# Loading k in natural key order, moving a mask to TensorE, and regrouping an output phase, in an attention + MoE kernel

## The chip, the cores and the metric

The kernel runs on one core of a Trainium2 chip. The metric is the time of one execution on the device, in microseconds (us). The lowest and the highest run of one kernel in one call lie 0.15% (e12b) to 0.83% (the changed kernel again) apart here, in e7b 1.1%; each run also lists the mean clock that was granted to TensorE. A change counts as faster or slower only from 2% on.

Engine names: PE is TensorE (matmuls) and PEld its weight loads, DVE is VectorE, ACT is ScalarE, POOL is GpSimd, and SP is SyncE. "Hardware queue" means a DMA queue fed by ACT or SP, and "software queue" the one fed by POOL. PSUM is the memory that the matmuls write; a "bank" is here one [128, 512] f32 slice of it, and the tiles named `s4` have four. A "stretch" is a piece of the execution between two marks. "First MoE matmul" always means the start of the first matmul on `w_in`.

## The reference

For 8 batches and 8 heads of size 64, 32 global and 512 local tokens attend. Global queries see all keys; local queries see the global keys and the local keys at a distance of at most 32. The result, transposed to tokens x 512, goes through a two-layer MLP. Cut to what matters:

```python
s_g = scale * q_g @ concat([k_g, k_l]).T                  # global rows
out_g = softmax(s_g) @ concat([v_g, v_l])
s_ll = where(abs(i - j) <= 32, scale * q_l @ k_l.T, -1e9) # banded local scores
s_l = concat([scale * q_l @ k_g.T, s_ll])
out_l = softmax(s_l) @ concat([v_g, v_l])
x = concat([out_g, out_l]).transpose(0, 2, 1, 3).reshape(B * S, H * D)
h = x @ w_in                                              # 512 -> 2048
return (h / (1 + exp(-1.702 * h))) @ w_out                # 2048 -> 512
```

## The kernel before

The program is scheduled by hand: every engine runs its instructions in the order in which they are written here. A "quad" is four heads of one batch, so there are 16 quads. After an opening, in which batch 0 gets its attention, MoE phases of 64 matmuls ("h" phases, `x @ w_in`) alternate with output phases of 64 matmuls ("o" phases, `g @ w_out`). The attention of the next batch is woven into these phases, mostly into the output phases. The first output phase and the second MoE phase are written out separately, and later ones come from one function.

The parts that the change touches (cuts marked with `# ...`):

```python
# k in 4-token rows; its partition order makes four loads of 64 KB per quad
kf = k_l.rearrange("b (u j) (c r t) d -> b j r u c (t d)", j=4, c=4, t=4)
def load_k(b, u, j):
    nc.gpsimd.dma_start(out=loaded[b][0][32 * j : 32 * j + 32, u], in_=kf[b, j][:, u])

# small global tiles of batch 0 in f32, cast later; v in two pieces (turned by 32 partitions)
def load_g32(b, names, hold=False, eng=None):
    for name, s in (("q", qgf), ("k", kgf), ("v", vgf)):
        if name in names:
            t = g32[b, name] = consts.tile([128, 2, D], F32, name="g32%s%d" % (name, b))
            if hold:                       # the load waits for this memset's engine
                nc.vector.memset(t[:, :, 0:1], 0.0)
            # ... issue on eng or nc.sync

q32 = ld.tile([128, 16 * D], F32, name="q32", bufs=1)
nc.scalar.dma_start(out=q32, in_=qf[0][:, 0])
load_g32(0, "qk")
load_g32(0, "v", eng=nc.scalar)            # small v tile: issued at once, on ACT's queue
for j in range(4):
    load_k(0, 0, j)
# ...
def Tk(self, cs=(0, 1, 2, 3)):             # k transpose: contiguous in, contiguous out
    # ...
    nc.vector.transpose(self.kT[:, cs], rk[:, cs])
def M(self, rnd, lo=0, hi=LW):             # mask: multiply exp(scores) by 0/1
    # ...
    nc.vector.tensor_mul(e, e, mask[:, rnd : rnd + 1, lo:hi].to_broadcast([128, 4, hi - lo]))
def R(self):                               # reciprocals of the sums: two transposes and a reciprocal
    # ...
def XL(self, h):                           # scaled outputs of the local rows -> x
    nc.vector.tensor_mul(self.x[:, 2 * self.u + h, :], self.st[1 + h], self.st["rs"])
def G(self):                               # global rows -> xG, needed only by the last MoE phase
    # ... reciprocal, multiply, transpose, reading self.st["og"]
```

The opening and the first output phase (`a` and `c` are two quads of one batch; S scores, X exp, M mask, ekU/U value matmuls, Gm the matmuls of the global rows, osteps the output matmuls):

```python
a.S(0); a.X(0); a.S(1, split=True, warm=4); a.X(1)   # written one per line in the kernel
c.ext(); cast_g32(0, "v"); c.Tk(); a.K(); a.XK(); a.M(0); c.Tq(); c.gg(); c.S(0); c.X(0); a.M(1)
# ...
a.ekU(1, 3); c.S(1); c.X(1, halves=True); a.ekU(2, 4); a.U(1); a.U(2); a.Gm(); c.M(0); a.XL(0)
# ...
# first output phase, its last third:
osteps(0, (3, 0)); a.U(1); a.U(2); c.S(1); a.Gm(); c.M(0); a.XL(0); a.XL(1)
c.X(1); c.M(1); c.eg(); a.G()
osteps(0, (3, 1), (3, 2))
c.UG(); c.RXG()                            # value matmuls, reciprocals, x, then G
osteps(0, (3, 3))
```

The softmax here doesn't subtract the row's maximum and nothing guards it: scores larger than these inputs give would overflow.

## Time and profile before

| Stage, read from the timeline of TensorE | us |
|---|---|
| start to the first MoE matmul | 20.19 |
| first MoE phase | 14.22 |
| first output phase, to the first matmul of the second MoE phase | 22.67 |
| second MoE phase, to the third one's start (with its output phase) | 36.02 |
| each later MoE phase with its output phase | 34.41 |
| span of the profiled execution | 310.7 |
| time, median of four runs (312.46 to 314.58) | 312.97 |

The page's busy row gives the engine, its busy time, its share of the span and its instructions:

```profile
PE 302.8 (97%) x3257; PEld 148.6 (48%) x3257; DVE 210.4 (68%) x463; ACT 167.3 (54%) x254; POOL 80.0 (26%) x131
```

TensorE is busy nearly all the time, so the change looks for its gain in the two stretches that do not run at the pace of the later phases: the opening, and the first output phase.

The timeline of before in the opening, TensorE only. Columns: start, duration, engine, line, operation with out<-in, tile, shape, type, count, and in brackets the idle time before it and its releaser:

```profile
8.49 1.04 PE L162 MATMUL s<-warm 128*128 128x512 bf16 x4
...
14.14 0.40 PE L367 MATMUL ov<-ek,rvg 32*32 32x512 bf16 x4
...
15.07 1.04 PE L162 MATMUL ov<-warm 128*128 128x512 bf16 x4
...
20.19 1.04 PE L457 MATMUL s<-xL,w_in_sb 128*128 128x512 bf16 x4
```

TensorE does useful work in small groups. The 11 matmuls on the tile `warm` after the first scores (two of their three groups are shown) compute nothing; they fill time in which TensorE would wait for exps and masks. The first value matmuls with global v (`ov<-ek,rvg`) run at 14.14 us.

The DMA view of before for the first 20 us. Columns: out<-in, issuing queue, kind and count, KB of each, and the median us from issue to landing:

```profile
q<-in_q_l_dram ACTq DMA_DIRECT2D x1, 512.0 KB, 3.9
...
g32v<-in_v_g_dram ACTq DMA_DIRECT2D x1, 48.0 KB, 4.2
g32v<-in_v_g_dram SPq DMA_DIRECT2D x1, 48.0 KB, 13.1
```

There are two loads named `g32v` because before also loads batch 1's small tiles early. Batch 0's, issued at 1.3 us, took 4.2 us. The same load for batch 1, issued at 14.1 us when the software queue was full of v and weights (its four 512 KB loads of `w_in`, issued from 10.4 us on, took 11.7 us in the median), took 13.1 us.

DVE's timeline of before at the end of the first output phase:

```profile
53.84 0.16 DVE L426 RECIPROCAL rg<-og 128x1 f32<-128x1 f32 x1
...
54.53 0.67 DVE L412 STREAM_TRANSPOSE sT<-ov 128x512 f32<-128x512 f32 x1
...
55.52 0.71 DVE L416 STREAM_TRANSPOSE rs<-rT 128x512 f32<-128x512 f32 x1
56.34 1.29 DVE L421 TENSOR_TENSOR xL<-ov,rs 128x512 bf16<-128x512 f32 x2
57.55 0.16 DVE L426 RECIPROCAL rg<-og 128x1 f32<-128x1 f32 x1
```

The reciprocal at 53.84 us begins quad a's G, which reads `og` in a bank of its own. The tail of the phase is sT, rT, rs and xL of quad c: xL ends at 57.63 us, 0.55 us after the second MoE phase began at 57.08 us. Quad c's G follows at 57.55 us and holds nobody up.

Finally, the groups of DVE transposes by form in before (busy us and mean ns of one):

```profile
L260 DVE STREAM_TRANSPOSE kT<-rk 128x512 f32<-128x512 f32 x15 | 10.6, 704 | 0.0
L263 DVE STREAM_TRANSPOSE q<-rq 128x512 f32<-128x512 f32 x15 | 10.2, 677 | 0.0
```

### The profile page before, as it was taken

The page shows a single profiled execution, that of the slowest core. Times are in us where ns is not written, and L with a number is a line of the kernel's source. Part 1 is how long each engine was busy: PE and PEld are TensorE (multiplying, and loading weights), DVE is VectorE, ACT ScalarE, POOL GpSimd, SP SyncE. Part 2 cuts the span into 40 slices and gives each one's busy share as a digit, 9 for nine tenths or more (in the row PEclk, how much of TensorE's full clock was granted, in tenths as well). Part 3 has the DMA queues.
Part 4 walks back from the last instruction along what each step waited for, and adds up shares of the span by engine and source line. Part 5 has one row for each costly group of instructions (what it writes and reads, how often), then busy time and mean ns, then how long its engine had stood idle before and what let it go on. Part 6 is the DMA issues. An engine that isn't in the chain of part 4 may idle for free.

```text
span 310.7 us, 7885 instructions
## 1 busy us (share of the span) xinstructions
PE 302.8 (97%) x3257; PEld 148.6 (48%) x3257; DVE 210.4 (68%) x463; ACT 167.3 (54%) x254; POOL 80.0 (26%) x131
## 2 busy tenths in 40 slices
PE   7899999999999999999999999999999999999995
PEld 6444444444554454444454455444454454446653
DVE  7887946869867866776957866776767855574320
ACT  4817465476536744565446735565556652563321
POOL 8822579677146000900045001200000000000000
PEclk9999999999999999999999999999999999999999
DMA  8999999999969212970279113901120012201123
GB/s 154 149 189 207 206 161 193 165 147 129 151 77 168 45 36 61 139 108 12 60 77 169 30 36 71 102 0 31 41 49 23 0 38 55 48 0 29 41 61 76
DMA packets 60099, 27.44 MB, mean 88 GB/s; under 512 B 43296, under 2 KB 51744, under 8 KB 60064
## 3 DMA queue, kind: packets, MB, share of 16 engines
q0 software_dynamic: 51536, 17.11, 50.7%
q1 hardware_dynamic: 7904, 9.12, 11.9%
q10 hardware_dynamic: 624, 0.72, 0.8%
q8 instruction: 25, 0.41, 0.5%
q14 instruction: 10, 0.08, 0.1%
HBM read 35.13 MB, written 8.91 MB: 142 GB/s over the span
## 4 chain that ended last, share of the span: by engine, by line
PE 91%; DVE 3%; ACT 2%; DMA 1%; POOL 1%; issue 0%; ACTq 0%; DVEq 0%; POOLq 0%
PE op L482 37%; PE hp L457 36%; PE s L291 6%; PE ov L389 5%; PE ov L367 3%; DMA rk<-in_k_l_dram 1%; PE s L457 1%; ACT e L322 1%; PE kb L310 1%; DVE e L329 1%; PE op L494 1%; PE s L310 1%; DVE gT L465 1%; PE s L406 1%; POOL rk L84 1%; PE ov L162 1%
## 5 line engine op out<-in xcount | busy, mean ns | idle before, releaser
L482 PE MATMUL op<-w_out_sb,gT 128*128 128x512 bf16 x528 | 121.9, 380 | 0.1
L465 DVE SCALAR_TENSOR_TENSOR gT<-th,hp 128x512 bf16<-128x512 f32 (+1 forms) x140 | 91.1, 655 | 43.0 <-ACT th L464 42.4
L457 PE MATMUL hp<-xL,w_in_sb 128*128 128x512 bf16 x496 | 108.6, 379 | 0.3 <-DVE xL L421 0.3
L464 ACT ACTIVATE th<-hp 128x512 f32<-128x512 f32 (+1 forms) x140 | 79.9, 573 | 43.7 <-PE hp L457 41.2
L457 PEld LDWEIGHTS <-w_in_sb 128*128 128x128 bf16 x576 | 56.1, 98 | 65.1 <-issue 1.2
L482 PEld LDWEIGHTS <-gT 128*128 128x128 bf16 x528 | 49.3, 98 | 56.2 <-issue 3.3
L322 ACT ACTIVATE e<-s 128x1712 bf16<-128x1712 f32 (+2 forms) x32 | 49.6, 1552 | 15.8 <-PE s L406 8.9
L496 ACT ACTIVATE ob<-op 128x512 f32<-128x512 f32 (+2 forms) x35 | 20.5, 585 | 61.6 <-PE op L482 59.1
L97 POOL DMA_DIRECT2D v<-in_v_l_dram x36 | 27.0, 757 | 96.2 <-PE s L406 88.9
L84 POOL DMA_DIRECT2D rk<-in_k_l_dram x64 | 34.9, 557 | 12.3 <-DMA w_in_sb<-in_moe_w_in_dram 4.7
L329 DVE TENSOR_TENSOR e<-e,mask 128x1408 bf16<-128x1408 bf16 (+2 forms) x33 | 28.0, 851 | 6.9 <-ACT e L322 6.7
L412 DVE STREAM_TRANSPOSE sT<-ov 128x512 f32<-128x512 f32 x16 | 11.4, 714 | 31.3 <-PE ov L389 31.3
L291 PE MATMUL s<-q,kT 32*128 32x200 bf16 (+1 forms) x512 | 21.3, 284 | 1.5 <-DVE kT L260 0.9
L421 DVE TENSOR_TENSOR xL<-ov,rs 128x512 bf16<-128x512 f32 x32 | 20.7, 685 | 2.2 <-PE ov L389 0.9
L291 PEld LDWEIGHTS <-kT 32*128 32x128 bf16 x512 | 10.9, 95 | 14.7 <-issue 9.1
L357 ACT ACTIVATE ek<-kb 128x512 bf16<-128x512 f32 x16 | 9.6, 600 | 8.4 <-PE kb L310 8.4
L389 PE MATMUL ov<-e,v 128*32 128x192 bf16 (+1 forms) x512 | 13.1, 240 | 0.0
L416 DVE STREAM_TRANSPOSE rs<-rT 128x512 f32<-128x512 f32 x16 | 11.4, 711 | 0.6
L260 DVE STREAM_TRANSPOSE kT<-rk 128x512 f32<-128x512 f32 (+1 forms) x17 | 11.4, 671 | 0.0
L263 DVE STREAM_TRANSPOSE q<-rq 128x512 f32<-128x512 f32 (+1 forms) x17 | 10.9, 647 | 0.0
L389 PEld LDWEIGHTS <-v 128*32 128x32 bf16 x512 | 9.8, 97 | 2.0 <-issue 2.0
L310 PE MATMUL kb<-q,kgT 32*32 32x512 bf16 x128 | 10.0, 385 | 0.5 <-ACT e L319 0.5
(71 smaller groups left out, 155.5 us busy)
## 6 DMA issues: line engine op xcount, KB each, us to landing
out_dram<-ob SPq DMA_DIRECT2D x132, 64.0 KB, 1.7
rk<-in_k_l_dram POOLq DMA_DIRECT2D x64, 64.0 KB, 4.0
v<-in_v_l_dram POOLq DMA_DIRECT2D x28, 128.0 KB, 4.5
rq<-in_q_l_dram POOLq DMA_DIRECT2D x6, 512.0 KB, 6.7
w_in_sb<-in_moe_w_in_dram POOLq DMA_DIRECT2D x4, 512.0 KB, 11.7
w_out_sb<-in_moe_w_out_dram POOLq DMA_DIRECT2D x4, 512.0 KB, 13.4
rq<-in_q_l_dram POOLq DMA_DIRECT2D x3, 256.0 KB, 7.9
q<-in_q_l_dram ACTq DMA_DIRECT2D x1, 512.0 KB, 3.9
```

Of the source, the lines that this page charges most:

```text
L84: nc.gpsimd.dma_start(out=loaded[b][0][32 * j : 32 * j + 32, u], in_=kf[b, j][:, u])
L97: nc.gpsimd.dma_start(out=vtiles[b % 2][p, s, :, :, :D], in_=vf[b, t][:, hs])
L291: nc.tensor.matmul(ps[j][:, off : off + n * nr], lhsT=self.k[p, 128 * c : 128 * c + 128, e], rhs=self.q[p, t0 : t0 + n, r0 : r0 + nr, e], ...
L322: nc.scalar.activation(e[:, :, lo:hi], self.ps[:, :, lo:hi], AF.Exp, scale=scale)
L329: nc.vector.tensor_mul(e, e, mask[:, rnd : rnd + 1, lo:hi].to_broadcast([128, 4, hi - lo]))
L389: nc.tensor.matmul(ov[32 * j : 32 * j + 32, :].rearrange("p (t r) -> p t r", t=16)[:, :, r0 : r0 + nr], lhsT=lv, rhs=self.E[c // 2][:, j, ...
L421: nc.vector.tensor_mul(self.x[:, 2 * self.u + h, :], self.st[1 + h], self.st["rs"])
L457: nc.tensor.matmul(hp[:, : width(i)], lhsT=w_in_c[:, fc // 8, kc, fc % 8 // 2, :, fc % 2], rhs=(xL[i] if i < B else xG)[:, kc, :], start=( ...
L464: nc.scalar.activation(th[:, :n], hp[:, :n], AF.Tanh, scale=0.851)
L465: nc.vector.scalar_tensor_tensor(gTs[i][:, fc, :n], in0=th[:, :n], scalar=1.0, in1=hp[:, :n], op0=ALU.add, op1=ALU.mult)
L482: nc.tensor.matmul(op, lhsT=gTs[i][:, fc, tci * 128 : tci * 128 + 128], rhs=w_out_sb[:, fc, :], start=(first and fc == 4 * f4), stop=(fc = ...
L496: nc.scalar.activation(ob[:, lo:hi], op[:, lo:hi], AF.Copy, scale=0.5)
```

## The change

The intent has four parts.

1. k is loaded like q, in 16-token rows of 2 KB on the software queue, which makes one load per pair of quads in place of eight. Keys come out in natural order only if the k transpose writes with a step (`"p (r t) -> p t r"`, a step of 16 f32 = 64 bytes).
2. k and q of the first quad come as f32 on the two hardware queues and are cast on chip.
3. In batch 0 the mask becomes a bias (0 or -262144) that an identity matmul adds to the scores in PSUM ahead of the score matmuls, in place of a multiplication after the exp.
4. The first output phase is regrouped so that matmuls of one tile size stand together.

On the way, the small v tile's load moves behind a DVE memset (`hold=True`) on SP's queue, constants move to POOL, and quad 1's loads leave the software queue earlier. The diff has more that the list leaves out: v's loads follow the new order of the keys, the first half of `w_in` comes in four loads in place of two, batch 1's small tiles come on the software queue, and the warm-up matmuls at the very start go from 62 to 40.

The diff, cut to its core:

```diff
-    kf = k_l.rearrange("b (u j) (c r t) d -> b j r u c (t d)", j=4, c=4, t=4)
+    kf = k_l.rearrange("b (u j) (r t) d -> b (j r) u (t d)", j=4, t=16)
 # ... load_k and load_q replaced by two whole loads
-    nc.scalar.dma_start(out=q32, in_=qf[0][:, 0])
-    load_g32(0, "qk")
-    load_g32(0, "v", eng=nc.scalar)
-    for j in range(4):
-        load_k(0, 0, j)
+    load_g32("q", qgf)
+    for eng, f in ((nc.scalar, halves[0]), (nc.sync, halves[1])):
+        eng.dma_start(out=k32[:, f], in_=kf[0][:, 0, f])
+        eng.dma_start(out=q32[:, f], in_=qf[0][:, 0, f])
+    load_g32("k", kgf)
 # ... constants on POOL, the band matrix, identity and bias
-            nc.vector.transpose(self.kT[:, cs], rk[:, cs])
+            nc.vector.transpose(self.kT.rearrange("p (r t) -> p t r", t=16)[:, lo:hi],
+                                loaded[self.b][0][:, self.u].bitcast(F32)[:, 32 * lo : 32 * hi])
+        def B(self, rnd, split=False):
+            # ...
+                for j in range(4):
+                    nc.tensor.matmul(ps[j][:, w : w + 16 * WIN[c][1]], lhsT=ident, rhs=near(bias, c),
+                                     start=(c == 2 * rnd), stop=False, skip_group_check=True)
 # ... opening
+    load_g32("v", vgf, hold=True)
+    cast_g32("k", rkg)
     transpose_g(0, 2, "k")
     load_rest()
+    a.B(0)
+    a.B(1, split=True)
+    a.S(0, added=True, part=0)
+    a.S(0, added=True, part=1)
     a.X(0)
-    a.S(1, split=True, warm=4)
+    a.S(1, split=True, added=True)
     a.X(1)
 # ... no a.M, no c.M in batch 0; value matmuls without warm-up matmuls
 # ... first output phase, last third
+    for unit in range(3):
+        a.U(unit)
+    a.R()
+    c.M(1)
+    c.eg()
+    pt = psS.tile([128, 4, 512], F32, name="s4")
+    a.Gm(pt[:, 0, 0 : D + 2])
+    osteps(0, (3, 0), (3, 1))
     a.XL(0)
     a.XL(1)
+    c.ekUs(banks=[pt[:, unit + 1, :] for unit in range(3)])
+    for unit in range(3):
+        c.U(unit)
     a.G()
-    osteps(0, (3, 1), (3, 2))
-    c.UG()
-    c.RXG()
-    osteps(0, (3, 3))
+    c.R()
+    c.XL(0)
+    c.XL(1)
+    c.Gm()
+    osteps(0, (3, 2), (3, 3))
 # ... quad c's G now runs in the second MoE phase, at step 1; the next batch's scores at step 10, not 9
```

## The prediction

> **What bounds the kernel now.** TensorE: the page's busy row has it at 302.8 of 310.7 us, the chain of waits is 91% TensorE, and from 93 us on that chain is matmul groups end to end. Two stretches are not at that pace.
>
> (a) Opening. In the timeline the first MoE matmul starts at 20.19 us. Ahead of it the chain runs: k DMA landing at 7.06 (issued by POOL at 1.35), q and k transposes, first scores at 7.90, exp 8.61-10.2, a chain through masks (0.89 us each), exps (1.6-1.8 us) and 11 warm-up matmuls of 512 columns, the last exp ending 16.85, the last mask 18.46, then 1.7 us of value matmuls.
>
> (b) First output phase: 34.41 to 57.08 us, 22.7 us in the table by stretches, against 20.6 us for the later phases (72.59-93.20, 107.0-127.6), which run the same counts (about 321 matmuls). So it holds at most 2.1 us. The chain there has an ACT exp (0.61), an exp/mask/DVE chain from 51.3 to 57.04, and the timeline shows roughly 0.2 us wherever tile sizes change. [...]
>
> **What changes, costed.**
> - k and q of quad 0 come on hardware queues as f32. q (512 KB) took 3.9 us that way; with 1 MB plus small tiles the queue moves about 384 KB/us (table by stretches, 3-4 us), so I estimate landings of 3.7-5.5 us. Casts: ACT 3 x 0.6 us, DVE one. The chain then sits on DVE: g32q (landed 5.1), its cast, transposes and copies. Scores complete at about 8.0-8.3 instead of 8.56: 0.2-0.7 us saved.
> - Batch-0 masks go: four DVE multiplies (3.5 us) out. 32 bias matmuls, 2 x 1408 columns per quad: about 0.6 us per round; three of four rounds fall into idle TensorE, the last (quad 1, round 1) sits between one exp and the next, because its PSUM tile is single-buffered: 0.6 us back on the chain. The exps now bound the opening: 1.6+1.8+0.6+1.8+0.6 us, ending about 17.1 (16.85 before), but the 1.6 us from there to the last mask goes. First MoE matmul at about 19.0: **1.1 us saved** (0.3-2).
> - Mask building (1.3 us ACT) moves into the first h phase, where ACT has 0.26 us spare per step. Free.
> - Regrouped output phase: about 21.0-21.3 us: **1.5 us saved**.
> - k loads in 2 KB rows: fewer packets, shorter POOL issue. DMA is off the chain after the opening: about 0.
> - k transposes now write with a 64-byte step; 16 of 0.70 us. [...] DVE has slack in the later phases (68% busy).
>
> From 93 us on: unchanged.
>
> **Prediction: 310.1 us**, 8 in 10 between 308.2 and 312.3. Faster by over 2%: 0.05; within 2%: 0.92; slower: 0.03.
>
> **What would show it.** First MoE matmul near 19.0 (was 20.19); scores ending near 8.2; no mask multiply in batch 0; ACT near continuous from 8.2 to 17; first output phase about 21.2 us; each later h plus output period still 34.4 us; k transposes still about 0.70 us.
>
> **What would make it wrong.** Strided k transposes much slower (delaying scores in every phase); g32q or k landing later because 1 MB shares the DMA engines; POOL's memsets delaying the band mask and the next loads, so that quad 1, v or w_in come late; bias matmuls running in a cold clock or serialising; a late drain of the regrouped phase before the next h phase. A bigger gain needs scores below 7.5 us.

The stages come to a gain of 2.7 us (1.2 at the first MoE matmul, 20.19 to 19.0, and 1.5 in the output phase), and 310.1 us lies 2.9 us below the median of before. The 0.6 us for a round of bias matmuls is an estimate that follows from the trace of before: 1408 columns at 0.22 us for 512, from start to start. In after, one round took 0.69 us (10.18 us to the next group at 10.87), and the last one, during which the granted clock fell from 1.00 to 0.50, took 0.95 us (17.08 to 18.03). Issuing the k loads took POOL 34.9 us in before (64 of 557 ns) and 6.1 us in after (9 of 680 ns).

## The result

The changed kernel took 316.94 us (median of four runs, 316.60 to 317.31) against 312.97 us, a ratio of 1.0118 with a 95% interval of 1.0079 to 1.0157. A ratio here is the mean time of one kernel's runs over the mean of the other kernel's runs of the same rounds, so it is not quite the ratio of the medians. By the 2% line this is "the same", but the interval lies above 1: it is slower, by 4.0 us, and 4.6 us above the end of the range that I gave.

| Stage | before | after | predicted |
|---|---|---|---|
| first score matmul starts | 7.90 | 7.79 | |
| start to the first MoE matmul | 20.19 | 22.85 | 19.0 |
| first MoE phase | 14.22 | 14.20 | no change |
| first output phase | 22.67 | 21.78 | 21.2 |
| second MoE phase to the third one's start | 36.02 | 38.00 | no change |
| each later MoE + output phase | 34.41 | 34.41 | 34.4 |
| span | 310.7 | 314.9 | |

The second and the fifth row hold nearly the whole loss. Measured between the starts of the first and second output phase, the way most of the experiments below are read, before takes 38.78 us and after 39.88.

The busy row of after: TensorE's busy time is the same as before, and the span is 4.2 us longer, so in sum the added time is idle. (The busy times do not hold the same work: before has 11 warm-up matmuls in its opening, after has bias matmuls and, as shown below, some matmuls at half clock.)

```profile
PE 302.8 (96%) x3272; PEld 149.9 (48%) x3272; DVE 210.5 (67%) x447; ACT 167.5 (53%) x251; POOL 55.9 (18%) x90
```

What TensorE waited for in after, from the start to the first output matmul (view of waits; columns: waiting group, what released it, us in total, times, longest):

```profile
PE ov L372 <- DVE rvg L117: 3.1, 1, 3.1
```

The timeline of after, answering to the one of before:

```profile
7.79 1.17 PE L295 MATMUL s<-q,kT 32*128 32x120 bf16 x48
...
12.70 0.49 PE L394 MATMUL ov<-e,ones 128*32 128x160 bf16 x16
16.33 0.40 PE L372 MATMUL ov<-ek,rvg 32*32 32x512 bf16 x4 [3.14 <-DVE rvg L117]
...
22.85 1.47 PE L463 MATMUL s<-xL,w_in_sb 128*128 128x512 bf16 x6
```

The chain has a new link. The value matmuls with global v, which ran at 14.14 us before, start at 16.33 us, after 3.14 us in which TensorE did nothing at all. They waited for the cast of the small v tile, and that cast waited for its load. The DMA view of after for the first 20 us shows why:

```profile
q<-in_q_l_dram SPq DMA_DIRECT2D x1, 256.0 KB, 4.9
...
g32k<-in_k_g_dram SPq DMA_DIRECT2D x1, 64.0 KB, 4.7
g32v<-in_v_g_dram SPq DMA_DIRECT2D x1, 48.0 KB, 7.1
```

The tile's own view says that the two pieces of the load were issued at 8.2 and 8.6 us, behind the memset at 8.1 us, and landed 7.1 to 7.3 us later, at 16 us.

After this wait TensorE also ran slower. Stretches of after (columns: window, its length, busy us and instructions of PE, PEld, DVE, ACT and POOL, granted TensorE clock, DMA share, GB/s):

```profile
14.00:16.00 2.00, 0.00 (x0) 0.00 (x0) 0.00 (x0) 0.48 (x1) 0.71 (x1) 1.00 1.25 203
16.00:18.00 2.00, 1.67 (x28) 1.08 (x28) 1.88 (x5) 0.00 (x0) 1.09 (x2) 0.87 1.24 207
18.00:20.00 2.00, 2.00 (x41) 1.13 (x44) 0.76 (x2) 1.02 (x1) 0.70 (x1) 0.50 1.13 206
20.00:22.00 2.00, 2.00 (x68) 1.05 (x56) 1.22 (x2) 0.58 (x1) 0.71 (x1) 0.78 1.13 213
22.00:24.00 2.00, 2.00 (x38) 0.94 (x27) 1.93 (x6) 0.00 (x0) 0.53 (x1) 1.00 1.12 210
```

The granted clock was 0.50 from 18 to 20 us. From the first `ov<-ek,rvg` to the first MoE matmul, after took 6.52 us (16.33 to 22.85), and two later kernels with the same order of work, whose clock was 0.87 to 1.00 in that stretch, took 5.58 and 5.59 us (e1 and e2 below). So, by this comparison of profiles, some 0.9 us of the loss in the opening is the clock. The wait was 3.14 us long, and the granted clock was 0.50 from about 17.5 to 20.8 us, beginning 1.2 us after the wait ended. No length of wait shows as the condition: in other profiles the clock was 0.50 where the longest wait was 2.1 us (e5, 16 to 22 us), 1.9 us (e1, 12 to 14 us) or 1.2 us (e8, 14 to 16 us).

The tail of the first output phase, DVE's timeline in after:

```profile
54.73 1.28 DVE L427 TENSOR_TENSOR xL<-ov,rs 128x512 bf16<-128x512 f32 x2
57.05 0.17 DVE L432 RECIPROCAL rg<-s 128x1 f32<-128x1 f32 x1 [1.04 <-PE s L394]
...
57.75 0.68 DVE L418 STREAM_TRANSPOSE sT<-s 128x512 f32<-128x512 f32 x1
...
58.74 0.71 DVE L422 STREAM_TRANSPOSE rs<-rT 128x512 f32<-128x512 f32 x1
59.49 1.29 DVE L427 TENSOR_TENSOR xL<-s,rs 128x512 bf16<-128x512 f32 x2
```

As in before, quad a's G (the reciprocal at 57.05 us, then a multiplication and a transpose) stands ahead of quad c's sT, rT, rs and xL. But now the reciprocal was held up for 1.04 us, although the value it reads, quad a's, had been written by 53.2 us. It is released by a matmul of line 394, which is one of quad c's. Quad a's global rows sit in bank 0 of the same four-bank PSUM tile that quad c writes into in banks 1 to 3, so my reading is that the wait is for the tile as a whole. (An estimate from this trace: DVE was free at 56.0 us and the sums that sT reads were complete at about 56.4 us, so the wait held c's chain up by about 0.65 us, and G's place ahead of it by another 0.70 us.) The x of the second MoE phase is thus complete at 60.78 us, 1.95 us after that phase began (0.55 us in before), and TensorE waits. In the view of waits for the stretch between the two output phases of after:

```profile
PE hp L463 <- DVE xL L427: 1.0, 2, 0.8
PE s L295 <- DVE q L267: 0.8, 1, 0.8
```

Before had 0.3 us here in all, of the first kind.

The transposes of after by form:

```profile
L253 DVE STREAM_TRANSPOSE kT<-rk 128x512 f32<-128x512 f32 x15 | 15.6, 1041 | 0.0
...
L257 DVE STREAM_TRANSPOSE q<-rq 128x512 f32<-128x512 f32 x15 | 10.1, 670 | 0.0
```

The k transpose, which now writes with a step of 64 bytes, takes 1041 ns in place of 704, while the q transpose is unchanged.

### The profile page after: what moved, and what is told of

Same layout as the page of the kernel before. It is cut to its first block, busy times and chain, and to the rows that moved or that the text cites. A ratio compares the mean times of both kernels' runs of the same rounds, so it can differ in the third digit from the quotient of the medians.

```text
span 314.9 us, 7824 instructions
## 1 busy us (share of the span) xinstructions
PE 302.8 (96%) x3272; PEld 149.9 (48%) x3272; DVE 210.5 (67%) x447; ACT 167.5 (53%) x251; POOL 55.9 (18%) x90
## 2 busy tenths in 40 slices
DMA packets 53923, 27.60 MB, mean 88 GB/s; under 512 B 42496, under 2 KB 43776, under 8 KB 53888
## 4 chain that ended last, share of the span: by engine, by line
PE 88%; DVE 4%; DMA 4%; ACT 2%; issue 0%; ACTq 0%; SPq 0%; DVEq 0%
PE op L488 37%; PE hp L463 34%; PE s L295 6%; PE ov L394 5%; PE ov L372 3%; DMA g32v<-in_v_g_dram 2%; DMA k<-in_k_l_dram 1%; DVE gT L471 1%; PE s L463 1%; PE kb L314 1%; PE op L500 1%; PE s L314 1%; ACT th L470 1%; PE s L412 1%; ACT e L325 1%; DVE kT L253 0%
## 5 line engine op out<-in xcount | busy, mean ns | idle before, releaser
L488 PEld LDWEIGHTS <-gT 128*128 128x128 bf16 x528 | 49.2, 98 | 56.4 <-issue 3.5
L325 ACT ACTIVATE e<-s 128x1712 bf16<-128x1712 f32 x31 | 49.5, 1597 | 19.3 <-PE s L412 8.9
L89 POOL DMA_DIRECT2D v<-in_v_l_dram x32 | 23.8, 753 | 124.1 <-PE s L412 114.4
L332 DVE TENSOR_TENSOR e<-e,mask 128x1408 bf16<-128x1408 bf16 x28 | 24.4, 871 | 6.7 <-ACT e L325 6.7
L418 DVE STREAM_TRANSPOSE sT<-ov 128x512 f32<-128x512 f32 x15 | 10.7, 716 | 27.1 <-PE ov L394 27.1
L295 PE MATMUL s<-q,kT 32*128 32x228 bf16 (+5 forms) x528 | 21.3, 283 | 0.8 <-DVE q L267 0.8
L427 DVE TENSOR_TENSOR xL<-ov,rs 128x512 bf16<-128x512 f32 x30 | 19.4, 687 | 2.7 <-PE ov L394 1.4
L253 DVE STREAM_TRANSPOSE kT<-rk 128x512 f32<-128x512 f32 (+1 forms) x17 | 16.8, 990 | 1.2 <-ACT rk L521 1.2
L372 PE MATMUL ov<-ek,rvg 32*32 32x512 bf16 x120 | 9.8, 384 | 3.1 <-DVE rvg L117 3.1
L394 PE MATMUL ov<-e,v 128*32 128x160 bf16 (+1 forms) x480 | 12.6, 243 | 0.0
```

The costliest lines, as they stand in the source:

```text
L89: nc.gpsimd.dma_start(out=vtiles[b % 2][p, s, :, :, :D], in_=vf[b, g][:, hs])
L295: nc.tensor.matmul(ps[j][:, off : off + n], lhsT=self.k[p, 128 * c : 128 * c + 128, e], rhs=self.q[p, lo:hi, r0 : r0 + nr, e], start=(e == ...
L325: nc.scalar.activation(e[:, :, :RW], self.ps[:, :, :RW], AF.Exp, scale=scale)
L332: nc.vector.tensor_mul(e, e, mask[:, rnd : rnd + 1, :].to_broadcast([128, 4, LW]))
L372: nc.tensor.matmul(ov[32 * j : 32 * j + 32, :], lhsT=lv, rhs=self.ek[p], start=True, stop=False, skip_group_check=True)
L394: nc.tensor.matmul(ov[32 * j : 32 * j + 32, :].rearrange("p (t r) -> p t r", t=16)[:, :, r0 : r0 + nr], lhsT=lv, rhs=self.E[c // 2][:, j, ...
```

## The experiments

My theory after this reading had two main causes: (1) the small v tile comes late, because its load leaves behind a memset and then meets a full software queue; and (2) the tail of the regrouped phase, where G waits for the wrong quad. Rivals: the f32 loads, casts or bias matmuls of the new opening are the cause; the regrouping itself is; or the loss lies in the clock alone. Kernels of one call ran on one chip and share their runs of before. The four kernels of the third call (e7, e9, e10, e12) were at first taken by no chip and gave no result; they ran unchanged under new labels (those with a "b").

### The changed kernel again

No edit.

> The changed kernel once more, on the chip of the next three, so that they can be compared with it and not only with the kernel before. Every theory expects a ratio to before of 1.010 to 1.015 (about 317 us), the first MoE matmul near 22.9 us after a TensorE wait of about 3.3 us for the small v tile, and about 1.0 us of waits ahead of the second MoE phase.

Measured: 316.68 us (315.74 to 318.37), ratio 1.0110 [1.0054, 1.0167]. First MoE matmul at 23.83 us in this profile, first to second output phase 39.87 us. The result repeats. Its two executions with a mean granted clock of 0.989 took 317.55 and 318.37 us, and the two with 0.995 and 0.997 took 315.81 and 315.74. The opening of one and the same kernel thus varies by about a microsecond and more, and where it does, the granted clock varies with it.

### e1: the small v tile early

```diff
     load_g32("k", kgf)
+    load_g32("v", vgf)
 # ...
-    load_g32("v", vgf, hold=True)
```

> Only the loads of the small v tile (64 KB) go from behind the first scores (8.2 us) to the end of the opening loads on the same queue (about 2.7 us). Theory A (the tile is late only because it was asked for late and then queued behind the big loads): it lands before 8 us, the wait of 3.3 us and the half clock after it go, the first MoE matmul comes at about 18.9 us (22.9 in the changed kernel), total about 4 us less: 312.9 us, ratio to before 0.997 to 1.002. Rival B (the DMA engines are full in the opening, so that what was last is late whatever its place): the wait moves to the big v or to w_in, the first MoE matmul stays after 21 us, ratio 1.006 or more.

Measured: 313.41 us (312.68 to 314.20), ratio 1.0007 [0.9970, 1.0044]. First MoE matmul at 20.54 us. One line takes 3.3 us off on the same chip (316.68 to 313.41), and the wait of 3.1 us is gone. The first to the second output phase is unchanged at 39.86 us, as it should be. Theory 1 holds. A new wait shows instead: 1.9 us for the q transpose of the first quad's second half, so the opening is still not at 19 us.

### e2: the clock held up while TensorE waits

```diff
     a.R()
-    a.ekU(1)
+    a.ekU(1, 14)      # 14 warm-up matmuls of 512 columns in the wait
```

> The changed kernel with 14 dummy matmuls of 512 columns put into the wait for the small v tile, into the bank that the next group overwrites. The wait itself stays (the tile lands at about 16 us). Theory: the granted clock fell to 0.5 from 17.5 to 20.4 us because TensorE sat idle, and that cost about 1.0 us; with the dummies the clock stays 1.0 and the first MoE matmul comes at 21.7 to 22.1 us, ratio to before 1.007 to 1.011, about 1 us below the changed kernel. Rival: the low clock costs nothing (the exp on ACT bounds that stretch): no change, first MoE matmul at 22.9.

Measured: 316.69 us (315.53 to 317.80), ratio 1.0111 [1.0068, 1.0154]. The profile shows what I expected of it: clock 1.00 throughout, first MoE matmul at 21.63 us, and 1.2 us less in the span than after. The four timed runs do not show it: their median is that of the changed kernel. So the effect of the clock is seen in profiles only, about 0.9 to 1.2 us, and is not confirmed in the timed runs. (The profile also has a pause of 1.2 us in the output phase for which the trace names nothing.)

### e3: the tail of the first output phase

```diff
-    c.ekUs(banks=[pt[:, unit + 1, :] for unit in range(3)])
+    c.ekUs(banks=[None] + [pt[:, unit + 1, :] for unit in (1, 2)])
     for unit in range(3):
         c.U(unit)
-    a.G()
     c.R()
     c.XL(0)
     c.XL(1)
+    a.G()
```

Quad c's sums get a bank of their own, and G stands behind the x of quad c.

> The changed kernel with one bank moved in the first output phase: the sums of the second quad go to a PSUM tile of their own, and the reciprocal chain of that quad stands ahead of the global rows of the first. Theory: in the changed kernel both read the same four-bank tile and so wait for the last of its 60 matmuls (57.0 us), then stand one behind the other; with this edit the chain starts about 1.4 us earlier (right after the sums), the waits of 1.0 us ahead of the second MoE phase go, and the kernel is 1.0 to 1.6 us faster than the changed one, ratio to before 1.007 to 1.010. Rival: the tail is bound by the exp and mask of the second quad; then less than 0.4 us is won.

Measured: 316.27 us (315.40 to 317.29), ratio 1.0099 [1.0061, 1.0138]. First to second output phase 38.76 us in place of 39.87, first MoE matmul at 24.70 us. DVE's timeline of this kernel at the end of the phase:

```profile
58.40 0.72 DVE L418 STREAM_TRANSPOSE sT<-ov 128x512 f32<-128x512 f32 x1 [0.43 <-PE ov L394]
...
60.25 1.29 DVE L427 TENSOR_TENSOR xL<-s,rs 128x512 bf16<-128x512 f32 x2
61.45 0.16 DVE L432 RECIPROCAL rg<-s 128x1 f32<-128x1 f32 x1
```

G comes last, and TensorE's waits of 1.0 us on xL are gone. (The edit moves the sums and G together, so it shows that this tail was the cost, not which of the two, order or shared tile, would have been enough.) The profile gives back 1.1 us, the timed median only 0.4 us, with overlapping intervals. The noise of the opening (24.70 us here) was larger than the effect. Run e16 below settles this.

### e4: the old output phase in the changed kernel

```diff
 # first output phase as in the kernel before:
+    a.U(0); a.R(); osteps(0, (3, 0)); a.U(1); a.U(2)
 # ...
+    osteps(0, (3, 1), (3, 2))
+    c.UG()
+    c.RXG()
+    osteps(0, (3, 3))
```

> The changed kernel with the first output phase put back in the order of the kernel before; its opening stays the changed one. So far the stretch from the first output matmul to the first output matmul of the next phase took 38.8 us before and 39.9 us in three profiles of changed kernels. Theory (the regrouped order itself costs 1.1 us, through its uncovered tail): the stretch returns to 38.6 to 39.0 us. Rival (the slower k transposes or something else of the change costs it, not the order): it stays above 39.5. Total about 1 us under the changed kernel, ratio 1.006 to 1.010, within the noise of the opening.

Measured: 316.90 us (315.67 to 317.40), ratio 1.0111 [1.0066, 1.0155]. The phase is 22.68 us long again, and from the first to the second output phase it takes 39.05 us. The regrouping as written (39.88 us) therefore costs 0.8 us over the old order in the same kernel. With the tail repaired (38.76 us) it saves 0.3 us. Timed runs again do not resolve it under the late v tile.

### e5: the kernel before with its v tile late

```diff
     load_g32(0, "qk")
-    load_g32(0, "v", eng=nc.scalar)
 # ...
     transpose_g(0, 2, "k")
+    load_g32(0, "v", hold=True)
     load_rest()
 # ... and its cast moved to where after has it
```

> The kernel BEFORE with one thing of the change put in: the small v tile of the first batch is asked for behind the first scores on the other hardware queue (about 8.3 us) and cast after the second quad's transposes. Theory A (asking late is the cost, whatever the rest): it lands 6 to 9 us later, at 15 to 17 us, the value sums wait for it, and the first MoE matmul comes at 21.2 to 23 us instead of 20.2; the total rises by 1 to 3 us, ratio 1.003 to 1.010. Rival (the lateness came from the new loads of the change, such as k as f32): it lands before 12 us and nothing is lost.

Measured: 318.32 us (317.88 to 318.50), ratio 1.0159 [1.0113, 1.0205] (by the 2% line unclear, as the interval reaches above 1.02, but slower beyond doubt), first MoE matmul at 25.93 us. This is the reverse of e1, in a kernel that has nothing else of the change, and it costs 5 us, more than the 1 to 3 us that I had expected. The tile's view has the cast at 15.1 us, 2.5 us after DVE stood ready for it. The wait reaches TensorE by a slightly different way than in after: quad a's second mask stands behind the cast in DVE's order, and TensorE waits 2.1 us for that mask. Then the clock fell. Two stretches of this kernel:

```profile
14.00:16.00 2.00, 0.12 (x8) 0.00 (x0) 0.91 (x2) 1.51 (x3) 0.71 (x1) 0.82 1.54 187
...
20.00:22.00 2.00, 2.00 (x19) 0.53 (x21) 0.00 (x0) 1.14 (x2) 0.21 (x1) 0.50 1.11 201
```

The clock was 0.50 in all three stretches from 16 to 22 us, with TensorE busy again for most of the time. Of the 5.7 us by which the first MoE matmul comes later than in before, 0.8 us is a longer wait for quad 1's q (1.2 against 0.4 us), 2.1 us the wait behind the cast, and the remaining 2.8 us, by the timelines, come after it, in and behind the stretch with the half clock (my estimate). Late v is enough to make the loss, without the f32 loads, the bias matmuls or the regrouping.

### e6: both repairs

The edits of e1 and e3 together.

> The small v tile early and the separate bank in the tail, both. If the two causes add up: first MoE matmul at 19.9 to 20.9 us as with the first alone, stretch from output phase to output phase 38.7 to 38.9 us, total 311.4 to 312.8 us, ratio 0.995 to 1.000. If they are one cause seen twice: no better than the early load alone (ratio 1.0007).

Measured: 313.72 us (313.11 to 313.93), ratio 1.0011 [0.9973, 1.0050]. First to second output phase 38.69 us, but the first MoE matmul only at 21.39 us. The waits of TensorE in this opening:

```profile
PE s L296 <- DVE q L258: 1.8, 1, 1.8
...
PE s L315 <- DVE kgT L202: 1.4, 1, 1.4
```

q's second half landed 5.9 us after its issue, and the small k tile 8.3 us after its own; quad 1's loads left the software queue at 2.33 us, while those were still on their way (before: 4.46 us). That gave a third suspect: quad 1's early loads. The timed ratio is no better than e1's (1.0011 against 1.0007), so these runs do not show that the two repairs add up; the stretch between the output phases does, and e16 below shows the tail in timed runs.

The DMA view of e6 for the first 20 us:

```profile
q<-in_q_l_dram SPq DMA_DIRECT2D x1, 256.0 KB, 5.9
...
g32k<-in_k_g_dram SPq DMA_DIRECT2D x1, 64.0 KB, 8.3
```

### e8: e6 with more warm-up matmuls at the start

```diff
-    keep(40, psP.tile([128, 512], F32, name="w", tag="p"), 128)
+    keep(56, psP.tile([128, 512], F32, name="w", tag="p"), 128)
```

> As the run before it in this list, and 56 instead of 40 warm-up matmuls at the start (62 before the change). Theory: with 40, TensorE idles from about 6 to 8 us and the granted clock falls to 0.5 in some executions (0.66 in the mean from 10 to 15 us in the profile with the early load), which costs about 0.5 to 1.2 us there; with 56 the clock stays at 1.0, the first MoE matmul comes at 19.0 to 20.0 us and the times of the runs lie closer together, total 310.6 to 312 us, ratio 0.992 to 0.998. Rival: the exps and loads bound the opening, so the clock there costs nothing: as the run before.

Measured: 314.57 us (313.70 to 315.69), ratio 1.0044 [0.9998, 1.0090]. A miss: nothing got better. The first MoE matmul is at 21.47 us (e6: 21.39). The profile's first output phase took 23.48 us in place of 21.78, with a pause of 1.5 us for which the trace names nothing, as in e2, so its longer time is not the opening's alone. The clock still fell, a little later. Stretches of this kernel:

```profile
8.00:10.00 2.00, 1.37 (x50) 0.97 (x48) 0.88 (x5) 0.75 (x1) 0.86 (x2) 1.00 1.57 182
10.00:12.00 2.00, 1.09 (x20) 0.79 (x24) 1.62 (x8) 2.00 (x5) 0.77 (x2) 1.00 2.40 154
12.00:14.00 2.00, 1.68 (x40) 0.74 (x36) 0.98 (x4) 1.21 (x4) 1.41 (x2) 0.69 1.76 187
14.00:16.00 2.00, 2.00 (x40) 0.71 (x32) 0.59 (x1) 2.00 (x3) 1.18 (x2) 0.50 1.23 198
```

TensorE waited for at most 1.2 us at a time here, and the clock was halved all the same after 4 us in which it had been busy for 1.37 and 1.09 of each 2 us. In before it was busy for 1.06 of 2 us from 6 to 8 us and 1.14 from 10 to 12 us, with full stretches after each, and the clock stayed at 1.00. So in these profiles warm-up work ahead of the waits (e8) did not keep the clock up, and work inside the wait (e2) did.

### e7b: e6 with contiguous k transposes

```diff
-            nc.vector.transpose(self.kT.rearrange("p (r t) -> p t r", t=16)[:, lo:hi],
+            nc.vector.transpose(self.kT[:, 32 * lo : 32 * hi],
                                 loaded[self.b][0][:, self.u].bitcast(F32)[:, 32 * lo : 32 * hi])
```

This puts the keys in a wrong order, so the result is not right (the comparison's tolerance let it pass all the same). Only its time matters.

> WRONG RESULT ON PURPOSE: the kernel with the early small v tile and the separate bank, in which the k transposes write contiguously (keys then stand in the wrong order, the work is the same). Theory: the 64-byte step of the write is what makes the 128x512 k transpose take 1.00 us instead of 0.70 (0.60 instead of 0.41 for a half); here it returns to 0.70 and 0.41, which shortens the wait for q of 0.8 us ahead of the first scores in the second MoE phase by 0.3 us or more, and the opening by up to 0.4 us; total 0.3 to 0.8 us less than the kernel it is built on (ratio 1.0011). Rival: the slowness comes from the layout read, or from DMA traffic; then 1.00 us stays.

Measured: 312.19 us (311.04 to 314.44), ratio 0.9987 [0.9940, 1.0034]. The transposes by form:

```profile
L254 DVE STREAM_TRANSPOSE kT<-rk 128x512 f32<-128x512 f32 x15 | 10.5, 702 | 0.0
```

The step alone makes the difference between 702 ns here and the 1041 ns that after shows. From the first to the second output phase this kernel takes 38.39 us against 38.69 for e6, so 0.3 us of the regrouping's gain had gone there. In the later phases it costs nothing: from the second output phase to the end both take 237.84 us.

### e9b: e6 with DVE masks in place of bias matmuls

```diff
-    a.B(0)
-    a.B(1, split=True)
-    a.S(0, added=True, part=0)
+    a.S(0, part=0)
 # ...
+    a.M(0)
+    a.M(1)
 # ... and c.M(0), c.M(1); the mask built in the opening
```

> As the kernel with the early small v tile and the separate bank, but the masks of the first batch are multiplied on DVE again (no bias matmuls; masks built on ACT in the opening). It tells what the masks on TensorE are worth. Theory (they save the 1.3 us between the last exp and its last mask, and give 0.8 us back in the bias matmuls between two exps): with DVE masks the first MoE matmul comes 0.3 to 1.2 us later than in the kernel it is built on (20.5 to 21.4 us in two profiles), so 21 to 22.4 us, and total 0.3 to 1.2 us more. Rival (other waits bound the opening): no difference within 0.3 us, or even earlier.

Measured: 314.37 us (313.24 to 314.62), ratio 1.0041 [1.0020, 1.0063], first MoE matmul at 21.84 us (e6: 21.39). The last exp starts 1.2 us earlier (16.52 against 17.75 us), since no bias matmuls stand in its way, as I read it, but masks follow it. The first MoE matmul is 0.45 us later than in e6, and the ratios differ by 0.3%, but their intervals overlap, and this is not a clean pair: e9b waited 1.0 us longer for q (2.8 against 1.8 us), more than it came later, and its output phase was 0.46 us longer. So neither the sign nor the size of what the masks on TensorE are worth is shown.

### e10b: e6 with k of the first quad as bf16 on the software queue

```diff
-        eng.dma_start(out=k32[:, f], in_=kf[0][:, 0, f])
+    nc.gpsimd.dma_start(out=rk[:, 0], in_=kf[0][:, 0])
 # ... no f32 tile of k, no casts of it
```

> As the kernel with the early small v tile and the separate bank, but k of the first quad comes as bf16 over the software queue again (one load in natural order, ahead of all others of that queue), so that neither 512 KB of f32 nor two casts on ACT stand in the opening. Theory (the two hardware queues with 1.2 MB are what makes the second q half and the small k tile late, at 7.4 to 10.6 us): q lands before 5.5 us, the small k tile before 8 us, first scores start at 6.5 to 7.6 us instead of 8.3 to 8.6, first MoE matmul at 19.3 to 20.4 us, total 0.5 to 1.5 us less. Rival (the loads of the second quad compete, whatever the queue of k): first scores stay after 8 us.

Measured: 312.82 us (312.03 to 313.18), ratio 1.0002 [0.9986, 1.0019]. k landed at about 7.0 us, and the first scores came at 8.75 us (e6: 8.55). That is no difference that the profiles can tell: with k as f32 and quad 1's loads early, the first scores started at 8.30 us in e1 and 8.86 us in e7b. So k as f32 on hardware queues shows no gain here, and the rival of the expectation holds: the first scores stay after 8 us. The first MoE matmul was at 20.34 us, in an execution with a granted clock of 1.00.

### e12b: e6 with quad 1's loads held back

```diff
-    load(0, (1,))          # right after the band matrix
 # ...
     a.Tk(0, 8)
+    nc.vector.memset(rk[:, 1, 0:1], 0.0)
+    load(0, (1,))
     a.Tk(8, 16)
```

> As the kernel with the early small v tile and the separate bank, but the software queue's loads of the second quad wait for the first k transpose (issue at about 5.2 us instead of 2.3; the kernel before issued them at 4.5 to 7.3 us). Theory (these loads, asked for 2 us earlier than before, take DMA time from the second q half and the small k tile): q lands before 6.3 us and the small k tile before 7.5 us, first scores at 7.0 to 7.8 us instead of 8.3 to 8.6, no wait of 1.2 to 1.4 us for the small k tile, clock 1.0 through the opening, first MoE matmul at 18.8 to 20.0 us; total 311 to 312.5 us, ratio 0.993 to 0.998. Rival (the hardware queues slow themselves): no change in the first scores, and the second quad's come later.

Measured: 312.38 us (312.19 to 312.65), ratio 0.9985 [0.9970, 1.0000]. The DMA view of this kernel for the first 20 us, to be set beside that of after:

```profile
q<-in_q_l_dram SPq DMA_DIRECT2D x1, 256.0 KB, 4.3
...
g32k<-in_k_g_dram SPq DMA_DIRECT2D x1, 64.0 KB, 4.0
g32v<-in_v_g_dram SPq DMA_DIRECT2D x1, 48.0 KB, 3.7
```

In e6 the same three took 5.9, 8.3 and 8.4 us. The first scores start at 7.74 us and the first MoE matmul at 19.85 us. In the profile this opening is 0.34 us shorter than that of before, and the spread between runs is small, 0.46 us. The third suspect was real. The landing times say so beyond this pair: the small k tile took 4.0 to 4.5 us in all seven profiles with the hold, and 4.7 to 8.3 us in the ten with the early loads and k as f32. (The timed ratios alone, 0.9985 against e6's 1.0011, have intervals that overlap.)

### e15: the changed kernel with this hold alone

```diff
-    load(0, (1,))
 # ...
     a.Tk(0, 8)
+    nc.vector.memset(rk[:, 1, 0:1], 0.0)
+    load(0, (1,))
```

> The changed kernel with one edit: the software queue's loads of quad 1 are held back (behind a memset that follows the first casts) to about 5 us; the small v tile still leaves behind its own memset at about 8.2 us. Theory A (the late small v tile is the main cause; the early loads of quad 1 only delay the second half of q and the small k tile): those two land by about 6.3 and 7.4 us as in e12b_hold, but the first value matmuls still wait for the small v tile, whose cast still runs at 15 to 17 us, the first MoE matmul stays at 22 to 24 us, and the time stays at 1.005 to 1.013 of before. Rival B (the early loads of quad 1 are what delays the small v tile, by queueing ahead of it): its transfer takes 3 us or less, the cast runs by 12 us, the first MoE matmul is at 20 to 20.8 us, and the ratio is about 1.000.

Measured: 314.52 us (313.64 to 316.02), ratio 1.0049 [1.0018, 1.0081], first MoE matmul at 22.34 us. The wait for the small v tile:

```profile
PE ov L371 <- DVE rvg L117: 2.1, 1, 2.1
```

The load still took 6.0 to 6.3 us and its cast ran at 15.5 us. Rival B, that quad 1's early loads alone make it late, falls. What the load still meets from 8.7 us on are v and the weights on the software queue; no run took those away, so this part is argued. The loads of quad 1 have a cost of their own, though: holding them is worth roughly 2 us in the changed kernel (ratio 1.0049 against 1.0110 to 1.0118, on different chips). The small k tile landed at 6.8 us (issue at 2.3, 4.5 us to landing), before the 7.4 us that I had expected; its cast at 8.6 us stood behind other work of DVE and waited for no load. Note that the profile is of the slowest run: three of the six took 315.3 to 316.0 us, the other three, with clocks of 0.999 to 1.000, 313.6 to 313.7 us, and of those no trace was kept.

### e13: e12b with the next batch's scores later

```diff
-        if fc == 10:
+        if fc == 12:
             a.S(0)
 # ...
-        if fc == 13:
+        if fc == 15:
             a.M(0)
```

> e12b_hold with one edit: in every steady MoE phase written as in the second one, the scores of the next batch are issued after step 12 instead of 10 and their mask after step 15 instead of 13. Theory A (the 0.8 us for which TensorE waits on the q transposes in the second MoE phase is the slower strided k transpose and the moved global rows pushing the DVE back, so it is a matter of when the scores are asked for): that wait goes, the first to the second output phase takes 37.9 to 38.1 us (38.69 in e12b_hold), the ratio is 0.996. Rival B (the DVE is short of time over the whole phase): the wait only moves to the mask or to the h products, and the stretch stays at 38.5 us or more.

Measured: 312.10 us (311.97 to 312.44), ratio 0.9968 [0.9945, 0.9990]. First to second output phase 37.75 us, even a little below theory A's number, and the wait is gone from there. But the next stretch gives most of it back:

```profile
PE s L295 <- DVE q L267: 0.5, 1, 0.5
```

From the start of the second MoE phase to that of the third it is 36.51 us, against 36.81 in e12b and 36.02 before. So the gain is 0.3 us, not 0.9, and rival B is closer: DVE is short of time over both phases. The choice of the second output phase's start as a mark had hidden that.

### e14: e13 with a shorter hold

```diff
+    nc.vector.memset(rk[:, 1, 0:1], 0.0)   # now right after the cast of the small q tile
+    load(0, (1,))
```

> e13_later_scores with the loads of quad 1 held only until after the cast of the small q tile, about 1 us earlier. If the TensorE waits for the quad-1 copies in the opening (DVE 1.34 us for quad 1's k landing at 9.45 us) are the price of the hold, the first MoE matmul comes 0.3 to 0.8 us earlier than in e13_later_scores (about 19.3 us). If the earlier loads again slow the second half of q and the small k tile, those land 0.5 us or more later and the first MoE matmul does not move or comes later. Ratio between 0.994 and 0.998.

Measured: 312.68 us (311.71 to 313.72), ratio 0.9988 [0.9961, 1.0014]. The profile has the first MoE matmul at 19.12 us, as hoped (e13: 20.05; e12b and e18, with e13's opening, 19.85 and 19.44), and q and the small k tile land no later (4.6 and 4.3 us). But three of the six runs had a granted clock of 0.991 and took 312.57 to 313.72 us, so the longer hold looks like the steadier choice.

### e18, e16 and e17: what the output phase is worth in a quiet opening

e18 is e12b once more, as the base. e16 is e12b with the changed kernel's tail (the edit of e3 taken back). e17 is e12b with the first output phase of the kernel before (the edit of e4).

> The kernel of e12b_hold once more, as the base for the two others of this call, on the same chip: ratio 0.997 to 1.000, the stretch from the first output phase to the second 38.69 us, from the first output phase to the third MoE phase 58.6 us.

> e12b_hold without the repair of the output phase's tail: the changed kernel's order is back, with first quad's global rows and the second quad's sums in one four-bank tile. Theory A (the tail was the second mis-sized term and costs as much in the timed runs as in the profile): the stretch is 39.86 to 39.9 us, and the median lies 1.0 to 1.4 us above that of e18_hold_again. Rival B (the timed runs of earlier kernels, 313.7 with the repair and 313.4 without it, were right, and the wait is given back later): the medians differ by less than 0.5 us.

> e12b_hold with the first output phase of the kernel before in place of the regrouped one. If the regrouping with a repaired tail is worth only what the profiles show (58.60 us from the first output phase to the third MoE phase against 58.95 us): the median lies 0.2 to 0.6 us above that of e18_hold_again. If the 0.9 us that the regrouped phase itself saves is kept in the end: 0.8 to 1.2 us above. If the regrouping is worth nothing: within 0.1 us.

| | median us (range) | ratio to before | first output phase | first to second output phase | first output phase to third MoE phase |
|---|---|---|---|---|---|
| e18, regrouped, tail repaired | 312.04 (311.77 to 312.88) | 0.9971 [0.9949, 0.9993] | 21.78 | 38.68 | 58.58 |
| e16, regrouped, tail as in after | 314.01 (313.34 to 315.12) | 1.0031 [1.0006, 1.0055] | 21.77 | 39.86 | 59.77 |
| e17, order of before | 312.33 (312.20 to 312.66) | 0.9976 [0.9955, 0.9997] | 22.67 | 39.03 | 58.93 |

Waits of TensorE in e16:

```profile
PE hp L463 <- DVE xL L427: 1.0, 2, 0.8
PE s L463 <- DMA w_in_sb<-in_moe_w_in_dram: 1.0, 1, 1.0
```

The tail costs 1.2 us in the stretch, and 2.0 us in the timed median. That is more than the 1.0 to 1.4 us expected of theory A, and rival B (less than 0.5 us) falls. In the profiled run of e16 a wait of 1.0 us for w_in in the first MoE phase comes on top; whether its other runs had it too is open. The order of before against the regrouped one costs 0.29 us in the median and 0.35 us in the stretch, which agrees with the first of the three expectations; the ranges of the timed runs overlap, so the stretch carries this reading.

## Why the prediction was right or wrong

By its stages my prediction was a gain of 2.7 us (1.2 at the first MoE matmul, 1.5 in the output phase; the predicted time itself lies 2.9 us below the median of before), and I got a loss of 4.0 us. That the time stayed within 2%, to which I gave 0.92, is no merit, since the sign was wrong. In spans (310.7 to 314.9 us) the miss is 6.9 us: 3.85 us at the first MoE matmul (22.85 against 19.0), 2.6 us between the output phases (39.88 against 38.78 - 1.5), and the remainder after that, 0.46 us more than in before, which a variant of the kernel before shows too (e5: 237.87 us from the second output phase to the end, after 237.97, before 237.51).

**Wrong: "First MoE matmul at about 19.0: 1.1 us saved".** The step that failed is the list of what comes on the chain: exps and bias matmuls were there, the small v tile was not. The diff moved its load behind a memset at 8.1 us; its transfer took 7.2 us and TensorE stood still for 3.1 us, with a half clock afterwards worth, in the profiles, about 0.9 us more. e1 shows it (3.3 us back from one line), and e5 shows it the other way round (5 us lost in the kernel before). I had listed "quad 1, v or w_in come late" among the dangers, but as a matter of POOL's memsets, and did not look at when `g32v` is issued. The trace of before already held the price: the same load for batch 1, issued at 14.1 us on the same queue, took 13.1 us.

**Half right: "Scores complete at about 8.0-8.3 instead of 8.56: 0.2-0.7 us saved".** The first exp starts at 8.53 us in after and 8.61 us in before, so 0.1 us was saved. The loads of quad 1, now leaving at 2.3 us, held up q's second half and the small k tile, whether the v tile was early (e6) or late (e3 and e4: 8.1 and 8.3 us for the small k tile). e6 against e12b shows it: 5.9 and 8.3 us against 4.3 and 4.0 us to landing, and 0.8 us by the ratios (1.0011 against 0.9985, with overlapping intervals). With both set right, the first MoE matmul comes at 19.1 to 20.1 us (e14, e16, e18, e17, e12b, e13), 0.1 to 1.1 us before that of before. So the arithmetic for the rest of the chain was about right, mostly in the lower part of "0.3-2".

**Wrong: "Regrouped output phase: about 21.0-21.3 us: 1.5 us saved".** The phase itself did become shorter: 22.67 to 21.78 us with the same 320 matmuls. I count 20 changes of tile size between matmul groups in before's timeline and 14 in after's. Of the 0.89 us, 0.28 us is a wait that before had at the end, so a change of tile size costs about 0.1 us here. Single matmuls in the trace of before say the same: from the start of a 128x512 matmul to the next start it is 0.31 us across a change of tile size and 0.22 us within a group. I had read 0.2 us per change. What failed is the word "saved": I read the phase alone and did not ask what the next phase needs from it. G waited for the wrong quad, x was complete 1.95 us after the next phase began instead of 0.55 us, and TensorE paid 1.0 us (e3, e16). "A late drain of the regrouped phase before the next h phase" stood in my list of dangers, uncosted. Of the 0.9 us that remain with the tail repaired, only 0.3 us arrive (e17 against e18). The longer k transposes cost both kernels time there (e7b: 0.3 us) and so do not explain this difference. What differs is that in e18 quad c's G is done in the second MoE phase: up to the second output phase DVE is busy for 13.17 us there, against 12.48 in e17, and TensorE waits 0.8 us for q, against 0.4. No run moves this G alone, so that part is argued.

**Wrong: "k transposes still about 0.70 us".** They took 1.04 us. The 0.70 us was my estimate, carried over from the contiguous transposes of before (704 ns); no trace then showed one that writes with a step. The trace of after shows it (1041 ns), and e7b isolates it (702 ns without the step). The effect on the time is small (0.3 us, e7b), since DVE has slack from 93 us on, as I wrote (busy for 67% of the span in after; from the second output phase to the end 237.84 us with and without the step).

**Right.** No mask multiplication is left in batch 0; mask building in the first MoE phase is free (14.20 against 14.22 us); later phases are unchanged (34.41 us); DMA is off the chain after the opening, with 53,923 packets in place of 60,099 and no gain to be seen from it.

**Open.** How much of the opening's spread is the clock and how much the landing times: the two come together. What the masks on TensorE are worth by themselves. Why e16 costs more in the timed runs than its tail shows.

The best version, e12b and e18 (with e13 as good), runs at 312.04 to 312.38 us: 0.15% to 0.3% below the kernel before (by the 2% line the same), and 4.6 to 4.9 us below the changed one. So the change's ideas were worth about 0.9 us at most, nearly all of it in the opening (in e18's profile 0.75 us there, and 0.1 us from the first output phase to the third MoE phase: 58.58 against 58.69). What was lost came from two loads in the wrong place and from the tail of the output phase, where the shared tile and the order of G are not separated.

## What to carry to other kernels

When a diff moves a load, find its consumer and the time at which it will be issued, and price it with a load that the trace shows under the same traffic (13.1 us for the small v tile in before), not with one issued before that traffic (4.2 us). When a phase is regrouped, follow the values that it hands on to the next phase: a reader of a shared multi-bank tile may be held until the last writer of any bank is done, as the trace of after suggests (1.04 us of idle DVE). Judge a stage by the time to a mark that lies far enough behind it; a gain at a near mark may be given back before the next one.

## What the runs measured of the hardware

- A small load on a hardware queue: the small v tile, in pieces of 48 and 16 KB, took 3.4 to 3.7 us to landing with quad 1's loads held back (e12b), 7.1 to 7.3 us when issued at 8.2 and 8.6 us beside v and weights on the software queue (after), and batch 1's 13.1 to 13.2 us (before).
- A DVE transpose of 128x512 f32 that writes with a 64-byte step took 1041 ns (after) against 702 to 704 ns contiguous (e7b, before), half as much again, or 0.66 ns per column more.
- The granted clock: in e8 it was 0.50 from 14 to 16 us although TensorE never waited longer than 1.2 us at a time from 8 us on; it had been busy for 1.37 and 1.09 of 2 us in the two stretches from 8 to 12 us.
- A change of tile size on TensorE: six changes fewer were worth about 0.6 us (before to after), so about 0.1 us each (an estimate that single matmuls in before's trace bear out, 0.31 against 0.22 us from start to start).
- A wait on a PSUM tile of four banks: in after a read of bank 0 waited until matmuls into banks 1 to 3 were done, 1.04 us of idle DVE. That the wait is for the whole tile is a reading of one trace; no run separates the tile from the order, and it may come from how the program sets its waits rather than from the chip.
